# Keys and queries of the split units: each loaded once, to one half of the partitions, two units deep, with the order searched anew

## The chip, the core and the metric

The kernel runs on one core of a Trainium2 chip. The metric is the device time of one execution in microseconds (us), lower is better; the time of a kernel is the median of its runs.

## What is computed

Attention with random features (8 batches, 8 heads, 576 positions, head dimension 64, 128 features), and then a feed-forward layer on its output (4608 tokens, model width 512, inner width 2048, exact GELU), all in fp32. The reference, cut to what matters:

```
q_s, k_s = q * scale, k * scale               # scale = 64 ** -0.25
def phi(x):
    h = einsum('bhsd,md->bhsm', x, omega) - sum(x * x) / 2
    return exp(h - max(h)) / sqrt(m)
q_p, k_p = phi(q_s), phi(k_s)
kv, z = einsum('bhsm,bhsd->bhmd', k_p, v), sum(k_p, axis=2)
x = einsum('bhsm,bhmd->bhsd', q_p, kv) / (einsum('bhsm,bhm->bhs', q_p, z) + 1e-06)
x = x.transpose(0, 2, 1, 3).reshape(4608, 512)
h = x @ w_in
out = (0.5 * h * (1 + erf(h / sqrt(2)))) @ w_out
```

## The kernel before

**Units and blocks.** The attention is cut into 32 units of two heads (four units to a batch), the feed-forward layer into 18 blocks of 256 tokens. Units 0 to 7 are computed in plain fp32 while the weights are loaded. Units 8 to 31, the split units, run beside the feed-forward blocks: TensorE (PE) works through the matmuls of the blocks (`product`, L1201, and `mm2`, L1310 to L1312), and the few matmuls of the units stand between them. Blocks 15 to 17 follow when all units are done.

**A split unit.** `split_pre` loads the transposed keys and queries (64 dimensions by two heads by 576 positions each) into the one tile `xt`. It has 128 partitions, so the 64 dimensions fill a half of them. `load_dup` (L752) loads the keys twice, once to either half, and the queries twice; four DMAs of 288 KB a unit. Then ten tiles of up to 256 positions pass through a ring of three buffers `r`: ScalarE (ACT) rounds all 128 partitions to the high part in fp32r (`x_high`, a CAST, L953), and GpSimd (POOL) puts x minus the high part into the upper half of the buffer (`x_low`, L958). So the lower 64 partitions hold the high part and the upper 64 the low part, and one matmul over 128 partitions (`proj`, L966; `om` holds omega in both halves) adds both. ACT copies a part of the result (`proj_lo`, L970), VectorE (DVE) adds it and takes the maximum (`proj_add`, L975). When the five tiles of the keys or of the queries are through, POOL subtracts the maxima (`shift`, L979), ACT takes the exponential (L787), and the rest of the unit follows: the values in two parts (`v_a` on ACT, `v_b` on DVE, L995), the keys' features in two parts (`k_high` on POOL, L489; `k_low` on DVE, L1003), the products and the division (L1013, L857, L872). There is one buffer for the keys and one for the queries: those of the next unit can be loaded when the last `x_low` of this unit has read them.

**What sets the order.** The program is a list of operations, each with its engine. Every engine issues its operations in the order of a table `RANK`, one number for each operation. SyncE (SP) issues nearly all DMAs in one queue, in that order too: loads of keys, queries and values (`load_vst`, L755; `v_max` on DVE, L1035, reads them first), the transposes of the blocks' input (`block_turn`, L1183) and of the queries' features (`q_turn`, L989), and the stores (L1322). A DMA whose operands aren't ready holds back those behind it. The numbers that stand in the calls of `op` (a cost, and for DMAs `size` and `off`) are the planner's; they choose free buffers for PSUM tiles and add a few filling matmuls at the start, and otherwise cost nothing on the chip.

Of the kernel before, what the change touches and what calls it, by code (L numbers as in the profile page):

```python
# [15 lines left out]
ALU = mybir.AluOpType  # L16
# [19 lines left out]
RANK = (1, 0, 0, 0, 0, 1, 25, 0, 4, 6, 1, 2, 3, 3, 2, 3, 6, 5, 6, 9, 9, 8, 10, 7, 12, 23, 23, 3, 10, 15, 12, 16, 11, 14, 14, 21, 17, 24, 3, 5, 7, 2,  # L36
# [342 lines left out]
def favor_attention_ffn(ctx: ExitStack, tc: tile.TileContext, qT, kT, v, omT, w_in, w_out, out):  # L379
    nc = tc.nc  # L380
    B, H, D, S = qT.shape
    NJ = H // 2
# [366 lines left out]
    def load_dup(u, s):  # L749
        sv = (kT, qT)[s][u.b, 2 * u.j:2 * u.j + 2].rearrange("h d s -> d h s")  # L750
        for r in range(2):
            nc.sync.dma_start(xt[r * D:(r + 1) * D, s], sv)  # L752
# [194 lines left out]
    XG = [(a + g * P, a + min(g + 2, NT) * P) for a in (0, R2) for g in range(0, NT, 2)]  # L947
    NK = len(XG) // 2
    KG = [list(range(g, g + 2)) for a in (0, MID + 1) for g in range(a, a + MID, 2)] + [[MID]]

    def x_high(u, i):
        a, b = XG[i]
        nc.scalar.copy(G['r', u, i][:, 0:b - a], xf[:, a:b])  # L953
# [601 lines left out]
```

## Time and profile before

| | |
|---|---|
| time, median of 3 runs (lowest, highest) | 916.39 us (916.22, 916.94) |
| time of the profiled execution | 916.21 us |
| its span, from the first to the last instruction | 914.4 us |
| busy share: PE, ACT, DVE, POOL | 98%, 81%, 80%, 61% |
| DMA: bytes, share of the 16 engines | 98.95 MB, 47.1% |
| TensorE's granted clock | full speed throughout |

The time of an execution is its span and what lies around it, here 1.8 us. A busy share is the time in which an engine had an instruction under way; matmuls overlap in a pipeline, so PE counts as busy also where its matmuls come a little late. PE does the bulk of the work in nearly all of the span; what the other engines do costs time only where PE waits for it.

### The profile page before, as it was taken

To read this page: it belongs to the slowest core of one execution; us is meant where nothing else is said; L and a number is where in the kernel's file an instruction comes from. 1 tells how busy PE (TensorE), PEld (TensorE's weight loads), DVE (VectorE), ACT (ScalarE), POOL (GpSimd) and SP (SyncE) were. 2 spreads that over 40 slices of the span, in tenths; PEclk is the share of its full clock that TensorE was granted. 3 is DMA by queue.
4 is the path that set the end of the run, shared out by engine and by line. 5 is a ranking of instruction groups with operands and counts; after the bars stand their busy time and mean duration, and the time that the engine had idled before them with its cause. 6 is when DMAs were issued, how large, how long until landed. Compare 5 with 4: busy or idle time off the path is not lost.

```text
span 914.4 us, 26629 instructions
## 1 busy us (share of the span) xinstructions
PE 899.0 (98%) x10037; PEld 699.4 (76%) x10037; DVE 728.3 (80%) x2378; ACT 739.2 (81%) x1590; POOL 556.7 (61%) x809
## 2 busy tenths in 40 slices
PE   8999999999999999999999999999999999999998
PEld 6886777687767777777777777767877877679997
DVE  3877999988988898777767888788879777756665
ACT  6999888999998888987789878989898846555553
POOL 1355568777888566764468636887686416544432
PEclk9999999999999999999999999999999999999999
DMA  9866612649446663484354476384645231121200
GB/s 281 252 211 199 170 43 80 154 93 179 92 102 129 154 123 91 103 184 85 63 140 96 91 148 132 75 173 80 143 101 92 49 74 30 24 54 42 48 25 24
DMA packets 165168, 101.27 MB, mean 111 GB/s; under 512 B 132528, under 2 KB 141104, under 8 KB 165040
## 3 DMA queue, kind: packets, MB, share of 16 engines
q1 hardware_dynamic: 164672, 98.95, 47.1%
q8 instruction: 79, 1.29, 0.6%
q10 hardware_dynamic: 368, 0.62, 0.2%
q14 instruction: 49, 0.40, 0.1%
HBM read 60.36 MB, written 9.44 MB: 76 GB/s over the span
## 4 chain that ended last, share of the span: by engine, by line
PE 89%; ACT 5%; DVE 2%; DMA 2%; issue 1%; POOL 1%; SPq 0%; DVEq 0%; ACTq 0%; POOLq 0%
PE h L1201 33%; PE acc L1310 9%; PE acc L1311 9%; PE acc L1312 9%; PE at L966 5%; PE h L1188 3%; PE acc L1303 3%; PE acc L1265 3%; PE at L857 2%; PE at L1265 2%; PE at L1013 2%; PE at L847 1%; DMA xh<-xc 1%; PE h L794 1%; DMA raw<-in_w_in 1%
## 5 line engine op out<-in xcount | busy, mean ns | idle before, releaser
L958 POOL TENSOR_TENSOR r<-xt,r 64x256 fp32r<-64x256 f32 (+1 forms) x240 | 180.6, 763 | 108.8 <-ACT r L953 81.7
L1201 PE MATMUL h<-xh,w 128*128 128x128 f16 x3264 | 236.2, 219 | 0.0
L1201 PE MATMUL h<-xh,wih 128*128 128x128 f16 x1632 | 197.2, 220 | 1.5 <-DVE h L1218 1.1
L1201 PEld LDWEIGHTS <-w 128*128 128x128 f16 x3264 | 195.6, 98 | 2.8
L1310 PE MATMUL acc<-woh,gh 128*128 128x512 f16 x448 | 170.3, 380 | 0.0
L1311 PE MATMUL acc<-woh,gl 128*128 128x512 f16 x448 | 169.8, 379 | 0.4 <-DVE gl L1300 0.4
L1312 PE MATMUL acc<-wol,gh 128*128 128x512 f16 x448 | 169.8, 379 | 0.0
L1201 PE MATMUL h<-xh,wil 128*128 128x128 f16 x816 | 155.5, 219 | 0.0
L1201 PEld LDWEIGHTS <-wih 128*128 128x128 f16 x1632 | 138.6, 98 | 11.8 <-DVE h L1218 0.9
L1300 DVE SCALAR_TENSOR_TENSOR gl<-h,bs,gh 128x512 f16<-128x512 f32 x116 | 86.3, 746 | 31.8 <-ACT gh L1235 30.6
L966 PE MATMUL at<-om,r 128*128 128x256 f32 x432 | 103.7, 342 | 4.0 <-POOL r L958 2.6
L953 ACT CAST r<-xt 128x256 fp32r<-128x256 f32 (+1 forms) x240 | 90.9, 390 | 13.4 <-PE at L966 9.2
L970 ACT COPY lo<-at 128x256 f32<-128x256 f32 (+1 forms) x240 | 82.3, 354 | 18.0 <-PE at L966 13.6
L1226 ACT ACTIVATE h<-h,bs 128x512 f32<-128x512 f32 x116 | 77.1, 666 | 19.0 <-PE h L1201 15.9
L966 PEld LDWEIGHTS at<-om,r 128*128 128x128 f32 x432 | 70.3, 189 | 23.7 <-POOL r L958 3.7
L1208 ACT COPY g<-h 128x256 f32<-128x256 f32 x136 | 50.6, 373 | 45.8 <-PE h L1201 44.8
L1312 PEld LDWEIGHTS <-gh 128*128 128x128 f16 x464 | 45.4, 98 | 54.5
L1201 PEld LDWEIGHTS <-wil 128*128 128x128 f16 x816 | 80.0, 98 | 7.4 <-issue 1.8
L1235 ACT ACTIVATE gh<-h,bs 128x512 f16<-128x512 f32 x116 | 80.1, 692 | 4.6 <-PE acc L1312 3.4
L1310 PEld LDWEIGHTS <-gh 128*128 128x128 f16 x464 | 45.3, 98 | 35.1 <-issue 0.2
L1213 DVE TENSOR_TENSOR g<-h,g 128x128 f32<-128x128 f32 x136 | 38.8, 285 | 41.3 <-ACT g L1208 40.5
L1311 PEld LDWEIGHTS <-gl 128*128 128x128 f16 x464 | 45.5, 98 | 33.5 <-DVE gl L1300 0.7
(234 smaller groups left out, 2125.0 us busy)
## 6 DMA issues: line engine op xcount, KB each, us to landing
xt<-in_qT SPq DMA_DIRECT2D x56, 288.0 KB, 4.4
xt<-in_kT SPq DMA_DIRECT2D x54, 288.0 KB, 4.3
out_x<-o SPq DMA_DIRECT2D x35, 256.0 KB, 3.1
raw<-in_w_in SPq DMA_DIRECT2D x16, 512.0 KB, 6.2
raw<-in_w_out SPq DMA_DIRECT2D x16, 512.0 KB, 4.4
w<-in_v SPq DMA_DIRECT2D x24, 320.0 KB, 4.2
vt<-in_v SPq DMA_DIRECT2D x8, 320.0 KB, 6.7
qpad<-qc SPq DMA_TRANSPOSE x48, 3.7
```

The lines of the kernel that those rows point to most:

```text
L953: nc.scalar.copy(G['r', u, i][:, 0:b - a], xf[:, a:b])
L958: nc.gpsimd.tensor_tensor(r, xf[D:, a:b], r, op=ALU.subtract)
L966: nc.tensor.matmul(o[:, t], r[:, t * P:(t + 1) * P], om, start=True, stop=True)
L970: nc.scalar.copy(G['lo', u, i][:, 0:n], pp_k(u, i)[:, 0:n, 1])
L1201: nc.tensor.matmul(h, w[p], x[r], start=first and i + m == 0, stop=last and i == 1 and m == 2, skip_group_check=True)
L1208: nc.scalar.copy(G['sa', n, c], G['h', n, c][:, 0:2 * P])
L1226: nc.scalar.activation(h, h, AF.Gelu, scale=G['bs', n][:, 2:3])
L1235: nc.scalar.activation(G['gh', n, c], G['h', n, c], AF.Copy, scale=G['bs', n][:, 3:4])
L1300: nc.vector.scalar_tensor_tensor(G['gl', n, c], G['h', n, c], G['bs', n][:, 3:4], G['gh', n, c], op0=ALU.mult, op1=ALU.subtract)
L1310: nc.tensor.matmul(acc, gh, woh[:, f, c0:c1], start=f == 0, stop=False, skip_group_check=True)
L1311: nc.tensor.matmul(acc, gl, woh[:, f, c0:c1], start=False, stop=False, skip_group_check=True)
L1312: nc.tensor.matmul(acc, gh, wol[:, f, c0:c1], start=False, stop=f == NF - 1, skip_group_check=True)
```

## The change

The keys of a unit are loaded once, to the lower half of the partitions, the queries once, to the upper half (`load_one` in place of `load_dup`): two DMAs of 288 KB a unit instead of four, so 48 DMAs fewer. The space that this leaves holds a second unit: unit k uses the columns `k % 2`, so the loads of one unit wait for the unit before the last. `x_high` now works on 64 partitions, the half in which the data lie, and `x_low` reads that half and writes the low part to the other half of `r`. For the keys the high part is below and the low part above, as before; for the queries it is the other way round. An operation without an engine makes the first split unit's loads wait until all plain units have used `xt`. The planner's numbers for DMAs are changed (larger sizes for transposes, stores and values), and all of `RANK` is new. The instructions of PE are the same in number and shape, those of DVE and POOL too.

```diff
-RANK = (1, 0, 0, 0, 0, 1, 25, 0, 4, 6, 1, 2, 3, 3, 2, 3, 6, 5, 6, 9, 9, 8, 10, 7, 12, 23, 23, 3, 10, 15, 12, 16, 11, 14, 14, 21, 17, 24, 3, 5, 7, 2,
...
-    def load_dup(u, s):
+    def load_one(u, s):
         sv = (kT, qT)[s][u.b, 2 * u.j:2 * u.j + 2].rearrange("h d s -> d h s")
-        for r in range(2):
-            nc.sync.dma_start(xt[r * D:(r + 1) * D, s], sv)
+        nc.sync.dma_start(xt[s * D:(s + 1) * D, u.k % 2], sv)
...
+    def x_cols(u, i):
+        a, b = XG[i]
+        z = i // NK
+        x = xt[z * D:(z + 1) * D, u.k % 2].rearrange("p h s -> p (h s)")[:, a - z * R2:b - z * R2]
+        r = G['r', u, i][:, 0:b - a]
+        return x, r[z * D:(z + 1) * D], r[(1 - z) * D:(2 - z) * D]
+
     def x_high(u, i):
-        a, b = XG[i]
-        nc.scalar.copy(G['r', u, i][:, 0:b - a], xf[:, a:b])
+        x, hi, _ = x_cols(u, i)
+        nc.scalar.copy(hi, x)
 
     def x_low(u, i):
-        a, b = XG[i]
-        r = G['r', u, i][D:, 0:b - a]
-        nc.gpsimd.tensor_tensor(r, xf[D:, a:b], r, op=ALU.subtract)
+        x, hi, lo = x_cols(u, i)
+        nc.gpsimd.tensor_tensor(lo, x, hi, op=ALU.subtract)
...
-            op('SP', 0.5, load_vst, u, r=['vstf'], w=[u.vk], size=340e3, off=2.5)
+            op('SP', 0.5, load_vst, u, r=['vstf'], w=[u.vk], size=400e3, off=2.6)
...
-            op('SP', 1.45, load_dup, u, s, w=[('x', s, a) for a in range(2)], size=720e3, off=3.2)
+            op('SP', 0.75, load_one, u, s, w=[('xp', u.k % 2, s)], size=330e3, off=2.4)
...
-            xr, rk = [('x', i // NK, a) for a in range(2)], ('r', u, i)
+            xr, rk = [('xp', u.k % 2, i // NK)], ('r', u, i)
...
+                if not moved:
+                    op(None, 0, nothing, w=[(x, a, c) for x in ('x', 'xp') for a in range(2) for c in range(2)])
+                    moved = True
```

**The load of the keys of unit 27.** On SP before (the first row is the keys of unit 26, the row `in_kT` in the middle those of unit 27, the last those of unit 28; `w_71<-in_v` is a unit's values):

```order
L752 DMA xt<-in_kT 64x2x576 x2
L989 DMA_TRANSPOSE qpad<-qc 128x9x128
L1322 DMA out_x<-o 128x512 x2
L989 DMA_TRANSPOSE qpad<-qc 128x9x128
L752 DMA xt<-in_qT 64x2x576 x2
L1183 DMA_TRANSPOSE xh<-xc 128x12x128
L752 DMA xt<-in_kT 64x2x576 x2
L755 DMA w_71<-in_v 128x640
L752 DMA xt<-in_qT 64x2x576 x2
L1183 DMA_TRANSPOSE xh<-xc 128x16x128
L989 DMA_TRANSPOSE qpad<-qc 128x9x128 x2
L752 DMA xt<-in_kT 64x2x576 x2
```

The same place now (the first `in_kT` is unit 26, the row `in_kT` with x2 is units 27 and 28):

```order
L751 DMA xt<-in_kT 64x2x576
L994 DMA_TRANSPOSE qpad<-qc 128x9x128 x3
L751 DMA xt<-in_kT 64x2x576 x2
L1327 DMA out_x<-o 128x512
L1188 DMA_TRANSPOSE xh<-xc 128x12x128
L751 DMA xt<-in_qT 64x2x576
L1188 DMA_TRANSPOSE xh<-xc 128x16x128
L994 DMA_TRANSPOSE qpad<-qc 128x9x128 x2
```

The keys of unit 27 stood behind the block's transpose `xh` (128x12x128) and now stand ahead of it, and those of unit 28 moved past both block transposes and two of `qpad`.

**The first tile of unit 27 on ACT.** Before (the first CAST is the last tile of unit 26's queries, the second the first tile of unit 27's keys):

```order
L953 CAST r<-xt 128x128
L1235 ACTIVATE gh<-h,bs 128x512
L1020 COPY kvs<-at 128x128
L1175 ACTIVATE xc<-ts,bs 128x512 x2
L1026 ACTIVATE kvz<-at 128x2
L970 COPY lo<-at 128x256
L1029 ACTIVATE kvh<-kvz 128x130
L953 CAST r<-xt 128x256
L1235 ACTIVATE gh<-h,bs 128x512
```

And now:

```order
L987 ACTIVATE qc<-et 128x1152
L959 CAST r<-xt 64x128
L959 CAST r<-xt 64x256
L975 COPY lo<-at 128x256
L1231 ACTIVATE h<-h,bs 128x512
L975 COPY lo<-at 128x256
L1240 ACTIVATE gh<-h,bs 128x512
L1025 COPY kvs<-at 128x128
L959 CAST r<-xt 64x256
```

Seven instructions stood between the two tiles; now the first tile of unit 27 stands right behind the last of unit 26.

**The values of unit 26.** On SP before (the second `in_v` row here is unit 27, the first unit 26) and on DVE, where `vmax` is the maximum of unit 26's values:

```order
L752 DMA xt<-in_kT 64x2x576 x2
L1183 DMA_TRANSPOSE xh<-xc 128x12x128
L1322 DMA out_x<-o 128x512
L755 DMA w_71<-in_v 128x640
L752 DMA xt<-in_qT 64x2x576 x2
L989 DMA_TRANSPOSE qpad<-qc 128x9x128 x2
L755 DMA w_71<-in_v 128x640
```

```order
L995 SCALAR_TENSOR_TENSOR w_71<-w_71,vsc 128x10x64
L1035 TENSOR_REDUCE vmax<-w_71 128x1
L1300 SCALAR_TENSOR_TENSOR gl<-h,bs,gh 128x512
L1179 SCALAR_TENSOR_TENSOR xc<-ts,bs,xc 128x512
L975 ISA w_71,nm<-at,lo 128x128
```

Now, on SP (the first `in_v` is unit 25, the second unit 26) and on DVE:

```order
L1188 DMA_TRANSPOSE xh<-xc 128x12x128
L751 DMA xt<-in_kT 64x2x576
L754 DMA w_71<-in_v 128x640
L751 DMA xt<-in_qT 64x2x576
L1327 DMA out_x<-o 128x512
L754 DMA w_71<-in_v 128x640
L751 DMA xt<-in_kT 64x2x576
L1188 DMA_TRANSPOSE xh<-xc 128x16x128
```

```order
L1219 TENSOR_TENSOR h<-h,g 128x256
L1028 TENSOR_TENSOR kvz<-at,kvs 128x2x64
L1040 TENSOR_REDUCE vmax<-w_71 128x1
L1223 TENSOR_TENSOR h<-h,g 128x128
L1305 SCALAR_TENSOR_TENSOR gl<-h,bs,gh 128x512
```

The values of unit 26 were loaded behind the keys of unit 24; they now stand ahead of them. On DVE the maximum moved behind the sums `kvz` of a unit.

## Rows read from the trace of the kernel before

**Rows 1.** The page: its span, and each engine's busy time and instructions.

```profile
span 914.4 us, 26629 instructions
...
PE 899.0 (98%) x10037; PEld 699.4 (76%) x10037; DVE 728.3 (80%) x2378; ACT 739.2 (81%) x1590; POOL 556.7 (61%) x809
```

**Rows 2.** Stretches: length, busy PE, PEld, DVE, ACT, POOL, clock, DMA share, GB/s.

```profile
0.00:112.00 112.00, 107.77 (x809) 86.89 (x809) 83.87 (x204) 98.06 (x218) 49.64 (x47) 1.00 0.75 225
112.00:690.00 578.00, 571.41 (x6542) 434.05 (x6539) 487.50 (x1800) 508.97 (x1112) 405.85 (x595) 1.00 0.53 113
...
880.00:914.40 34.40, 30.15 (x380) 28.00 (x377) 20.50 (x46) 15.95 (x33) 10.75 (x18) 0.99 0.09 32
```

**Rows 3.** Waits of PE by what it waited for: total us, times, longest.

```profile
PE at L966 <- POOL r L958: 2.6, 3, 1.5
PE at L966 <- DVE nm L975: 1.4, 1, 1.4
```

**Rows 4.** Timeline, unit 27's first keys: start us, length, engine, instruction [idle before <-releaser].

```profile
597.47 1.29 SPq L752 DMA_DIRECT2D xt<-in_kT  x2
...
602.82 0.41 ACT L953 CAST r<-xt 128x256 fp32r<-128x256 f32 x1 [1.57 <-DMA xt<-in_kT]
...
607.51 3.27 POOL L958 TENSOR_TENSOR r<-xt,r 64x256 fp32r<-64x256 f32 x3
...
608.77 0.38 PE L1311 MATMUL acc<-woh,gl 128*128 128x512 f16 x1
608.98 0.38 PE L1312 MATMUL acc<-wol,gh 128*128 128x512 f16 x1
610.84 0.74 PE L966 MATMUL at<-om,r 128*128 128x256 f32 x4 [1.48 <-POOL r L958]
```

**Rows 5.** Timeline, the values of unit 26 on SP, DVE and PE.

```profile
531.58 0.42 SPq L755 DMA_DIRECT2D w<-in_v  x1
...
536.58 0.82 DVE L1035 TENSOR_REDUCE vmax<-w 128x1 f32<-128x640 f32 x1 [1.68 <-DMA w<-in_v]
...
540.33 0.23 PE L1201 MATMUL h<-xh,wih 128*128 128x128 f16 x1 [0.49 <-DVE h L1218]
...
543.13 0.19 PE L857 MATMUL at<-kvl,qpad 128*128 128x65 f16 x1 [0.31 <-DVE kvl L1032]
...
545.70 0.20 PE L857 MATMUL at<-kvh,qpad 128*128 128x65 f16 x1 [0.22 <-DVE xk L872]
```

**Rows 6.** Timeline, where DVE and POOL overlap, on POOL, DVE and PE.

```profile
549.37 0.88 DVE L995 SCALAR_TENSOR_TENSOR w<-w,vsc 128x640 f16<-128x640 f32 x1
...
556.17 0.22 PE L1201 MATMUL h<-xh,wih 128*128 128x128 f16 x1 [0.64 <-DVE h L1218]
...
683.15 2.11 POOL L979 TENSOR_TENSOR w<-w,nm 128x1152 f32<-128x1152 f32 x1
...
683.30 2.65 DVE L995 SCALAR_TENSOR_TENSOR w<-w,vsc 128x640 f16<-128x640 f32 x1 [0.24 <-ACT w L992]
...
686.71 0.36 PE L966 MATMUL at<-om,r 128*128 128x256 f32 x1 [1.35 <-DVE nm L975]
```

**Rows 7.** Timeline of PE, a wait in the keys of unit 14.

```profile
278.68 0.39 PE L966 MATMUL at<-om,r 128*128 128x256 f32 x1 [0.72 <-POOL r L958]
```

**Rows 8.** DMA: queue's packets, MB, share; issues by tile, KB each, us to landing; landing of L752.

```profile
q1 hardware_dynamic: 164672, 98.95, 47.1%
...
xt<-in_kT SPq DMA_DIRECT2D x54, 288.0 KB, 4.3
...
DMA to landing us min/median/max: 3.5/4.3/6.9
```

**Rows 9.** Groups by shape on POOL and timeline of ACT: work on fewer and more partitions.

```profile
L958 POOL TENSOR_TENSOR r<-xt,r 64x256 fp32r<-64x256 f32 x192 | 153.7, 807 | 81.2 <-ACT r L953 60.8 <-issue 7.9 <-POOL w L489 2.2
...
L1152 POOL TENSOR_TENSOR ts<-xk 128x256 f32<-128x256 f32 x34 | 27.5, 814 | 3.9 <-DVE w L617 1.7 <-DVE xc L1179 1.2
...
269.00 0.20 ACT L499 COPY bs<-bs 32x5 f32<-32x5 f32 x1
269.23 0.19 ACT L500 COPY bs<-bs 64x5 f32<-64x5 f32 x1
```

More of the change, by code (lines that the diff above doesn't have):

```diff
@@ L31 @@
 X = dict(pm=0.15, tsw=1.28, psw=0.057, pst=0.3, plain=8, tiles=6, fill=0.6, kvp=8, eb0=8, amax=0, ahead=4.5)
-RANK = (1, 0, 0, 0, 0, 1, 25, 0, 4, 6, 1, 2, 3, 3, 2, 3, 6, 5, 6, 9, 9, 8, 10, 7, 12, 23, 23, 3, 10, 15, 12, 16, 11, 14, 14, 21, 17, 24, 3, 5, 7, 2,
[173 rows of a table removed]
+RANK = (1, 0, 0, 0, 0, 1, 41, 0, 4, 6, 1, 2, 2, 3, 3, 3, 6, 6, 4, 9, 8, 8, 7, 7, 14, 17, 21, 3, 9, 16, 12, 19, 10, 15, 17, 24, 18, 26, 3, 5, 10, 2, 7,
[173 rows of a table added]
 PO = {}
@@ L1121, in split_post @@
         for a in range(2):
-            op('SP', 1.35, q_turn, u, a, r=[qc] + [qc + (1,)] * a, new=[(('qf', 'ql')[a], (('qf', 'ql')[a], u))], size=600e3, off=1.7)
+            op('SP', 1.35, q_turn, u, a, r=[qc] + [qc + (1,)] * a, new=[(('qf', 'ql')[a], (('qf', 'ql')[a], u))], size=740e3, off=1.7)
         out_ops(u)
@@ L1353, in block_prep @@
                 op('SP', 1.55, block_turn, n, k, r=[xc] + [xc + (q, l) for q in (p - 1, p) for l in range(2)] + [('xh', n)] * k, w=[('xh', n, k)],
-                   new=[] if k else [('xh', ('xh', n))], size=(800e3, 1060e3)[k], off=1.7)
+                   new=[] if k else [('xh', ('xh', n))], size=(950e3, 1250e3)[k], off=1.7)
     def ffn_first(n, c):
@@ L1416, in ffn_second @@
                             op('DVE', 0.12 + (min(c1, end) - c0) / 960, o_last, n, i, c0, min(c1, end), r=[('acc', n, 2 + i, 0)], w=[('o', n, i, c0)] + [('o', n, i)] * (n < NBLK - 1))
-                        op('SP', 0.45, store_dma, n, i, c0, c1, r=[('o', n, i), ('o', n, i, c0)], size=270e3 * (c1 - c0) / DM)
+                        op('SP', 0.45, store_dma, n, i, c0, c1, r=[('o', n, i), ('o', n, i, c0)], size=300e3 * (c1 - c0) / DM)
             return
@@ L1429, in ffn_second @@
                        new=[] if c0 else [('o', ('o', n, i))], due=(1, n + 1, (lag + i * .6) / nc_, 0.0), kind='F' if n >= N32 else 'F0')
-                    op('SP', 0.45, store_dma, n, i, c0, c1, r=[('o', n, i)], size=270e3 * (c1 - c0) / DM, due=(1, n + 1, (lag + 1) / nc_, 0.0))
+                    op('SP', 0.45, store_dma, n, i, c0, c1, r=[('o', n, i)], size=300e3 * (c1 - c0) / DM, due=(1, n + 1, (lag + 1) / nc_, 0.0))
     def p2():
@@ L1484, in favor_attention_ffn @@
     op('DVE', 0.2, vb_ones, w=['vb'])
-    done_u = NJ
+    done_u, moved = NJ, False
     for n in range(1, NBLK):
@@ L1501, in favor_attention_ffn @@
         if n == min(SB):
-            op(None, 0, nothing, w=[('et', e, t) for e in range(2) for t in range(2 * NT)] + [('x', a, c) for a in range(2) for c in range(2)]
+            op(None, 0, nothing, w=[('et', e, t) for e in range(2) for t in range(2 * NT)] + [('xp', a, c) for a in range(2) for c in range(2)]
                + [('vst', i) for i in range(NVS)] + ['kk', 'vb', 'tgf'] + [('kk', g) for g in range(len(KG))])
```

346 rows, old and new, of the table RANK are left out of this document.

## The prediction

> **What bounds the kernel now.** I read the page first, then PE busy time by stretches, then PE's waits, then the timeline ahead of each wait, back to what was late first. The page says that PE is busy for 899.0 us of a span of 914.4 us [rows 1]. The other engines are at 61% to 81%, so their work costs time only where PE stands still for it. The change leaves PE's instructions as they are in number and shape; all that it can win or lose is in the 15.4 us in which PE isn't busy, and in how late matmuls come inside the busy time.
>
> By stretches [rows 2]: in the first 112 us (plain units, weights) PE lacks 112.00 - 107.77 = 4.23 us, most of it at the very start. From 112 to 690 us, where the split units run beside the blocks, it lacks 578.00 - 571.41 = 6.59 us. From 880 us it lacks 34.40 - 30.15 = 4.25 us, the last store's way out. The change works in the middle stretch, so 6.59 us is what it can win there as idle time. An idle stretch costs a little more than it is long: ahead of the wait at 610.84 us PE's matmuls start 0.21 us apart (608.77, 608.98), and the next one starts 1.86 us later [rows 4]. That is 1.65 us lost for 1.48 us shown; I add 0.16 us to each wait. Some 14 waits make the most that the middle can give 6.59 + 14 x 0.16 = 8.8 us (an estimate; the count is mine from the timeline).
>
> Who is waited for: `proj` for the subtraction on POOL, 2.6 us in three waits, and for DVE's maxima, 1.4 us in one [rows 3]. Both are ends of chains, so I went back in time from the largest.
>
> Chain 1, 1.48 us at 610.84 us [rows 4]. The keys of unit 27 are issued at 597.47 us. ACT reaches their first tile and stands 1.57 us until 602.82 us for the DMA. POOL's subtractions for the following tiles end at 607.51 + 3.27 = 610.78 us, and PE goes on 0.06 us later. A DMA was late by about as much as PE then waited.
>
> Chain 2, 0.49 + 0.31 + 0.22 us from 540.33 us [rows 5]. The values of unit 26 are issued at 531.58 us; DVE stands 1.68 us for them until 536.58 us, and what is queued behind (the sums `h` that PE needs, then `kvl`, then the division) is late three times.
>
> Two others have nothing to do with loads [rows 6]. At 683.15 us POOL begins a `shift` of 2.11 us, and DVE's `v_b`, which takes 0.88 us at 549.37 us, takes 2.65 us from 683.30 us. PE then waits 1.35 us at 686.71 us. The 0.64 us at 556.17 us stands likewise behind a DVE instruction beside a `shift`. The 0.72 us at 278.68 us [rows 7] I couldn't trace to one cause.
>
> **The change part by part.**
>
> Removed: 48 of the 96 loads of 288 KB, 48 x 0.295 = 14.2 MB of the 98.95 MB on the queue, one seventh; the DMA engines are busy 47.1% [rows 8]. By itself that is worth nothing, since no load is on PE's path but through the two chains. For those it matters: loads land 3.5 to 6.9 us after issue, 4.3 in the median [rows 8], and the pair of 597.47 us took over 5 us.
>
> Moved, on SP and ACT: the order shows the keys of unit 27 ahead of the block's transpose that they stood behind; with a second buffer nothing forbids that. SP then goes past no new wait for a buffer, since the unit before the last has been read long ago. The keys of chain 1 were 1.57 us late. Now they are one load instead of a pair, whose issue alone holds SP for 1.29 us [rows 4], and the transpose that held them back stands behind them; I judge that to be more than 1.57 us, and take chain 1 away whole: 1.48 + 0.16 = 1.64 us. The same on ACT: the first tile of unit 27 now comes right behind the last of unit 26, seven instructions earlier, so that a late load there would again hold up ACT; it would have to be late by those seven too.
>
> The values of unit 26 stand ahead of the keys of unit 24 now, and DVE takes their maximum after more work. I take chain 2 away whole: 0.49 + 0.31 + 0.22 + 3 x 0.16 = 1.50 us. What is late next in either place is the ordinary mix, which I leave as it is.
>
> Changed in kind: 240 CASTs on ACT cover 64 partitions instead of 128, and 240 subtractions on POOL write to the other half. Length goes by the columns, not the partitions: POOL's tensor_tensor over 256 columns takes 807 ns on 64 partitions and 814 ns on 128, ACT's copy of 5 columns 0.20 us on 32 and 0.19 us on 64 [rows 9]. So nothing for ACT; a gain is excluded by that row. For POOL no row shows a write to other partitions than those read. I take nothing, since it is the same operation over the same columns; the bounds are nothing and twice the 807 ns (below). What covers it: POOL is busy 405.85 of 578 us [rows 2].
>
> The wait before the first split unit: its loads now wait for all plain units' queries too. It lies ahead of 112 us, where PE has the plain feed-forward block to do, and PE shows no wait for those loads; nothing, or the few tenths of a small wait.
>
> Everything else is the new order: who stands beside whom in 112 to 690 us is drawn again. The waits that aren't from loads, 6.59 - 1.48 - 1.02 = 4.09 us, may shrink or grow; I take them as equal, as I do the start's 4.23 us and the end. The largest is of a kind the order still holds: a `v_b` somewhere beside a `shift`.
>
> Sum: 916.21 us (this execution) - 1.64 - 1.50 = 913.07 us. It lies 0.18 us below the median of the runs, which gives **913.2 us**. I call under 0.2% (1.8 us) no change, about what a measurement of this kernel can tell.
>
> **The rivals.**
>
> *The loads are gone but other waits take their place: about 915.8 us.* Four waits of chain 2's sort, 0.5 us each with its 0.16, give back 4 x 0.66 = 2.6 us. For it: 4 us of the middle's idle time has no load in it, and PE at 99% is waiting for whoever is last. Against it: the two largest load waits are named and both have a place in the order that moved.
>
> *DVE behind `shift`: slower.* POOL runs 48 shifts of 2.1 us; two of them now end in a wait of PE, 1.35 and 0.64 us, mean 1.0 and 1.15 us with its start-up. The Trainium skill (SBUF — State Buffer, "Who interferes with whom") says that a VectorE instruction with two SBUF inputs and a GpSimd instruction that reads SBUF exclude each other for the whole instruction, whoever came first; this trace agrees, with 2.65 us in place of 0.88. Where the new order leaves n shifts with PE's next operand behind them, the time is 913.2 + (n - 2) x 1.15. It comes out above 918.2 us, slower by over 0.2%, from n = 7; at n = 8 it is 920.1 us. For it: the same pair, `v_b` and `shift`, stands in every unit. Against it: only two of 48 cost PE anything.
>
> *The subtraction across halves is slow.* If a write to the other half took twice 807 ns, POOL would have 240 x 0.8 = 194 us more; 405.85 + 194 = 600 us doesn't fit in the 578 us of the middle. POOL would be the bound there, and 22 us plus the waits of a full engine would be added: some 945 us. The Trainium skill (GPSIMD Engine Reference, "Extended-addressing connectivity") speaks for it: in a tensor_tensor each core works on its own 16 partitions. No run here shows such a write.
>
> *More than the loads' waits goes.* If an order with later loads no more in its way also halves the other 4.09 us: 913.2 - 2.0 - 0.16 x 4 = 910.5 us; with all gone, 908 us.
>
> **How the numbers follow.** Load waits gone, the rest as before, 912 to 914.5: 0.38. More gone, 908 to 912: 0.20. Given back, 914.6 to 918.2: 0.24. Shifts, 918.2 to 921: 0.14. POOL slow: 0.04. So faster by over 0.2% is 0.38 + 0.20 = 0.58, within 0.2% is 0.24, slower 0.18. The likeliest alone is 912 to 914.5 us. The range runs from 908.5, near the most that the middle can give (916.4 - 8.8 = 907.6), to 919.0: it leaves out the slow POOL, most of the shifts' case, and a few in a hundred below.
>
> **What would show it.** Right: ACT no longer waits for `xt` from 112 to 690 us; DVE's wait for values is gone; PE's idle time in the middle stretch falls from 6.6 to about 4 us; POOL's subtraction of 256 columns stays near 807 ns. Wrong: PE's waits behind DVE (`nm`, `h`, `gl`) grow beside a `shift`; POOL's subtraction is longer; ACT waits for `xt` at tiles that were moved forward; or the start loses more than 4.2 us, since pieces of the weights and values there are in another order too.

## The result, and the profile after

The changed kernel takes 923.17 us (median of 4 runs, 922.41 to 924.62) against 916.31 us for the kernel before in the same comparison: a ratio of 1.0076, 95% interval 1.0058 to 1.0093. It is slower by 6.9 us where 913.2 us was predicted, and lies outside the range. The profiled execution took 922.41 us.

The head of the page of the changed kernel, which answers to [rows 1]:

```profile
span 920.6 us, 26586 instructions
...
PE 903.4 (98%) x10037; PEld 703.2 (76%) x10037; DVE 732.6 (80%) x2378; ACT 756.0 (82%) x1590; POOL 557.9 (61%) x809
```

The counts of PE, ACT, DVE and POOL are those of before, and one figure stands out: ACT is busy for 756.0 us, 16.8 us more than the 739.2 us of [rows 1], with the same 1590 instructions. DVE and PE gained about 4 us each, POOL 1. I had costed the change at nothing for ACT.

The stretches of [rows 2] after (us, busy us of each engine with its instructions, granted clock, DMA share, GB/s):

```profile
0.00:112.00 112.00, 108.15 (x787) 87.46 (x788) 78.84 (x201) 95.61 (x213) 48.84 (x48) 0.97 0.77 225
112.00:690.00 578.00, 569.10 (x6478) 431.99 (x6477) 489.92 (x1778) 520.47 (x1100) 401.76 (x588) 1.00 0.41 90
```

Two things: in the first 112 us the granted clock is 0.97 where it was full before, and in the middle PE lacks 578.00 - 569.10 = 8.90 us where it lacked 6.59 us, instead of the 4 us that I expected. To place the loss I set the k-th matmul of each kind in the one trace against the k-th of the same kind in the other. The first matmul of the plain feed-forward block starts 2.95 us later (57.6 us in before), the matmul that started at 159.6 us still 2.96 us later, the last one 6.23 us later. So about 3.0 us are lost in the first 58 us, nothing from there to 159.6 us, and 3.3 us behind that. The 3.0 us are not idle time: in the first 112 us PE lacks 112.00 - 108.15 = 3.85 us, less than the 4.23 us of before.

The start, by single microseconds (us, PE busy us with its matmuls, granted clock, DMA share, GB/s):

```profile
14.00:15.00 1.00, 0.11 (x2) 1.00 1.10 375
15.00:16.00 1.00, 1.00 (x9) 0.85 1.13 294
16.00:17.00 1.00, 1.00 (x6) 0.50 1.07 270
...
21.00:22.00 1.00, 1.00 (x8) 0.50 0.14 51
22.00:23.00 1.00, 1.00 (x8) 0.74 0.00 0
23.00:24.00 1.00, 1.00 (x11) 1.00 0.00 0
```

From 15.7 to 22.5 us TensorE runs at 0.50, the lower of its two levels (1.2 GHz), and gets 6 to 8 matmuls done in a microsecond. Before, the same microseconds, behind a wait as long (0.91 us, to 0.89 us after), are at 1.00, with 11 matmuls:

```profile
14.00:15.00 1.00, 0.10 (x1) 1.00 1.12 383
15.00:16.00 1.00, 0.99 (x9) 1.00 1.06 344
16.00:17.00 1.00, 1.00 (x11) 1.00 1.08 389
```

PE's waits in the middle (us in total, times, longest), which answer to [rows 3]:

```profile
PE h L1206 <- DVE h L1223: 3.0, 3, 1.4
PE acc L1316 <- DVE gl L1305: 1.2, 1, 1.2
PE at L971 <- POOL r L963: 1.1, 2, 0.9
PE at L1018 <- DVE nm L980: 0.8, 1, 0.8
PE h L1206 <- DVE gl L1305: 0.8, 2, 0.5
```

The waits for POOL's subtraction have gone down from 2.6 to 1.1 us, and DVE no longer waits for values; the load chains of the prediction are gone. ACT still waits for keys once, 2.2 us at the first split unit (until 121.73 us), and PE has no wait behind it. Waits for DVE have taken their place. The largest, 1.24 us at 581.89 us and 1.42 us at 605.54 us, look like the rival "DVE behind `shift`". DVE at the first of them:

```profile
578.95 0.43 DVE L1219 TENSOR_TENSOR h<-h,g 128x256 f32<-128x256 f32 x1
579.29 2.34 DVE L1008 SCALAR_TENSOR_TENSOR w<-w 128x256 f16<-128x256 f32 x1
581.55 0.28 DVE L1223 TENSOR_TENSOR h<-h,g 128x128 f32<-128x128 f32 x1
```

and POOL beside it:

```profile
579.24 2.11 POOL L984 TENSOR_TENSOR et<-et,nm 128x1152 f32<-128x1152 f32 x1
```

The split of the keys' features (`k_low`, L1008), 0.42 us in the median of its kind, takes 2.34 us, and the addition that PE needs stands behind it. So my first theory, **O**, was that the new order costs the time, at the start by the clock and in the middle by DVE beside POOL. Its rival, **L**, was that the loads, or the write to the other half, cost it.

### The profile page after: what moved, and what is told of

It is laid out like the page before. It is cut to its first block, busy times and chain, and to the rows that moved or that the text cites. A ratio compares the mean times of both kernels' runs of the same rounds, so it can differ in the third digit from the quotient of the medians.

```text
span 920.6 us, 26586 instructions
## 1 busy us (share of the span) xinstructions
PE 903.4 (98%) x10037; PEld 703.2 (76%) x10037; DVE 732.6 (80%) x2378; ACT 756.0 (82%) x1590; POOL 557.9 (61%) x809
## 4 chain that ended last, share of the span: by engine, by line
PE 83%; ACT 8%; DVE 4%; issue 2%; DMA 2%; POOL 1%; SPq 0%; DVEq 0%; ACTq 0%; POOLq 0%
PE h L1206 30%; PE acc L1315 8%; PE acc L1316 8%; PE acc L1317 8%; PE at L971 5%; PE h L1193 3%; PE acc L1308 3%; PE acc L1270 3%; PE at L1270 2%; PE at L1018 2%; PE at L856 2%; PE at L846 1%; PE h L793 1%; ACT r L959 1%; ACT lo L975 1%
## 5 line engine op out<-in xcount | busy, mean ns | idle before, releaser
L963 POOL TENSOR_TENSOR r<-xt,r 64x256 fp32r<-64x256 f32 (+1 forms) x240 | 176.3, 743 | 103.3 <-ACT r L959 65.4
L971 PE MATMUL at<-om,r 128*128 128x256 f32 x432 | 106.1, 346 | 2.0 <-POOL r L963 1.1
L959 ACT CAST r<-xt 64x256 fp32r<-64x256 f32 (+1 forms) x240 | 89.5, 381 | 17.7 <-PE at L971 8.8
L975 ACT COPY lo<-at 128x256 f32<-128x256 f32 (+1 forms) x240 | 80.4, 350 | 8.7 <-PE at L971 3.1
L980 DVE CUSTOM_DVE_ANT_0 w<-at,lo 128x128 f32<-128x128 f32 x198 | 48.8, 285 | 20.4 <-ACT lo L975 19.0
```

Source lines behind the costliest of these rows:

```text
L959: nc.scalar.copy(hi, x)
L963: nc.gpsimd.tensor_tensor(lo, x, hi, op=ALU.subtract)
L971: nc.tensor.matmul(o[:, t], r[:, t * P:(t + 1) * P], om, start=True, stop=True)
L975: nc.scalar.copy(G['lo', u, i][:, 0:n], pp_k(u, i)[:, 0:n, 1])
```

## The experiments

The runs were made in four groups: e1 to e5, e6 to e9, e10 to e13, e14 to e16. Each group has runs of the kernel before, with medians of 916.1 to 917.1 us; the ratios and their 95% intervals are to those. Differences between my kernels are those of their medians, so across groups a difference below 1 us isn't certain.

**e1_loads_only**: the new loads, and every engine in the order of before.

```diff
-RANK = (1, 0, 0, 0, 0, 1, 41, 0, 4, 6, 1, 2, 2, 3, 3, 3,
+RANK = (1, 0, 0, 0, 0, 1, 25, 0, 4, 6, 1, 2, 3, 3, 2, 3,
...
```

> The new loads with the order of before: every engine issues its work in the order of the kernel before, and only what the loads and the split write is new. Theory O (the new order costs the time, the loads do not): the load waits of before (1.48 us at 610.84, 1.02 us between 540 and 546) go at least in part, the clock stays at 1.00 throughout, 913.5 to 916.5 us. Theory L (the loads or the write to the other half cost it): 920 to 923 us.

Measured: 924.45 us (923.47 to 925.35), 1.0079 times before, 1.0064 to 1.0094. Theory O falls: with the order of before the kernel is as slow as the changed one. Two of the five runs have a mean clock of 0.995 (925.3 us), three 0.999 (923.5 to 924.5 us); the clock is the smaller part here. Since the order is the same, every instruction has its counterpart in before, and the lateness could be followed along ACT. It grows by some 0.12 us at a time, mostly at a query's CAST and at the instruction right behind it (185 of the 243 steps above 0.08 us). These are the rows of ACT in the changed kernel where that shows, a cast of a key piece first (lower half), then one of a query piece (upper half):

```profile
594.61 0.28 ACT L959 CAST r<-xt 64x128 fp32r<-64x128 f32 x1
594.80 0.36 ACT L1213 COPY g<-h 128x256 f32<-128x256 f32 x1
595.06 0.36 ACT L975 COPY lo<-at 128x256 f32<-128x256 f32 x1
595.45 0.40 ACT L959 CAST r<-xt 64x256 fp32r<-64x256 f32 x1
595.88 0.37 ACT L975 COPY lo<-at 128x256 f32<-128x256 f32 x1
```

The first number is the start, the second the length. Behind the key cast the next instruction starts at 594.80 us, 0.09 us before the cast's end at 594.89 us. The query cast waits for the end of the COPY ahead of it (595.06 + 0.36 = 595.42, then 0.03 us), and the COPY behind it waits for the cast's end (595.85, then 0.03 us). In before, with casts over 128 partitions:

```profile
217.99 0.39 ACT L953 CAST r<-xt 128x256 fp32r<-128x256 f32 x1
218.28 0.36 ACT L970 COPY lo<-at 128x256 f32<-128x256 f32 x1
218.55 0.40 ACT L953 CAST r<-xt 128x256 fp32r<-128x256 f32 x1
```

That is a CAST every 0.56 us with a COPY between. I then took all pairs of the changed kernel in which ACT did not have to wait (at most 40 ns idle). A cast on the lower half starts 104 ns before the end of a neighbour on all partitions (median; 84 of 89 overlap), and the neighbour behind it 97 ns before the cast's end (82 of 83). For casts on the upper half both are 24 ns behind the end (none of 94 and none of 89 overlap). Two casts on the upper half in a row overlap again (9 of 9, by 93 ns). So the length of an instruction is what I said, 0.40 us in either kernel; its price is not: 104 + 24 + 97 + 24 = 249 ns more for each of the 120 query casts, at most 30 us of ACT's time. This is theory **S**. Its rival **W** is that POOL and DVE waiting for each other cost the time whatever ACT does.

**e8_upper_cast** and **e9_lower_cast** test that in the kernel before, with its loads and its order, where both halves of `xt` hold the same data. The diff is that of e8; e9 has `:D` and `D:` exchanged in the new lines.

```diff
     def x_high(u, i):
         a, b = XG[i]
-        nc.scalar.copy(G['r', u, i][:, 0:b - a], xf[:, a:b])
+        nc.scalar.copy(G['r', u, i][D:, 0:b - a], xf[D:, a:b])

     def x_low(u, i):
         a, b = XG[i]
-        r = G['r', u, i][D:, 0:b - a]
-        nc.gpsimd.tensor_tensor(r, xf[D:, a:b], r, op=ALU.subtract)
+        r = G['r', u, i][:, 0:b - a]
+        nc.gpsimd.tensor_tensor(r[:D], xf[D:, a:b], r[D:], op=ALU.subtract)
```

> The kernel before (its loads, its order), but every one of its 240 casts runs on partitions 64 to 127 alone, and POOL writes the low part to partitions 0 to 63. Theory S: twice as many such casts as in e1_loads_only, so about twice its 7.2 us: 926 to 933 us. If a half cast costs ACT nothing: 916 to 917.5 us.

> The kernel before, but every one of its 240 casts runs on partitions 0 to 63 alone, and POOL reads there and writes the low part to partitions 64 to 127. Theory S: casts that begin at partition 0 overlap as before, and POOL's write to the other half costs nothing: 916 to 917.5 us. If any half cast, or POOL's write to the other half, costs: as e8_upper_cast.

Measured: e8 934.65 us (1.0194, 1.0179 to 1.0209), e9 915.81 us (0.9992, 0.9983 to 1.0001). The two differ in nothing but the half, by 18.8 us for 240 casts. ACT in e8:

```profile
221.32 0.40 ACT L953 CAST r<-xt 64x256 fp32r<-64x256 f32 x1
221.74 0.37 ACT L970 COPY lo<-at 128x256 f32<-128x256 f32 x1
222.14 0.40 ACT L953 CAST r<-xt 64x256 fp32r<-64x256 f32 x1
```

and in e9, at the same place of the program:

```profile
217.79 0.39 ACT L953 CAST r<-xt 64x256 fp32r<-64x256 f32 x1
218.08 0.36 ACT L970 COPY lo<-at 128x256 f32<-128x256 f32 x1
218.35 0.40 ACT L953 CAST r<-xt 64x256 fp32r<-64x256 f32 x1
```

A cast and a copy take 0.82 us in e8 and 0.56 us in e9. Theory S is shown, and POOL's write to the other half, which both have, costs nothing: e9 is no slower than before. That POOL writes up in the one and down in the other makes no difference either: a subtraction takes 747 ns in e8 and 756 ns in e9.

**e7_old_order_full_cast** takes the price out of e1_loads_only: the query cast covers all 128 partitions (the lower half of what it writes is overwritten by POOL's low part), and six matmuls keep the clock up (e4_fill_wait, below).

```diff
     def x_high(u, i):
         x, hi, _ = x_cols(u, i)
+        if i >= NK:
+            a, b = XG[i]
+            x, hi = xt[:, u.k % 2].rearrange("p h s -> p (h s)")[:, a - R2:b - R2], G['r', u, i][:, 0:b - a]
         nc.scalar.copy(hi, x)
```

> The new loads with the order of before, as e1_loads_only, with the cast of the queries over 128 partitions and the six matmuls at 14 us. Theory S: of the 7.2 us that e1_loads_only lost behind 160 us nearly all comes back, and the loads give at most the 1.6 + 1.0 us of the waits that they end: 914 to 917 us. Rival W, or loads that cost by themselves: 921 to 924 us.

Measured: 915.51 us (0.9991, 0.9982 to 1.0000), 8.9 us below e1_loads_only, or 8.1 us by the two ratios. The new loads by themselves are worth 0.6 us, and the interval reaches from nothing to 1.6 us. ACT's wait of 1.57 us at the head of chain 1 is gone, but PE's wait there is still 0.78 us long after 1.48 us: 3 us later ACT waits 1.20 us for DVE's `dn` (the denominators of the division).

**e3_old_start** and **e4_fill_wait** are about the start. e3 issues what the changed kernel planned for its first 58 us in the order of before, the rest in the new one; here the first rows of SP that this moves:

```diff
 L743 DMA vt_74<-in_v 128x10x64
-L559 DMA raw<-in_w_in 128x4x256 x2
-L747 DMA xt<-in_kT 128x576 x2
 L743 DMA vt_75<-in_v 128x10x64
 L559 DMA raw<-in_w_in 128x4x256 x2
-L747 DMA xt<-in_qT 128x576
 L747 DMA xt<-in_kT 128x576
+L747 DMA xt<-in_qT 128x576 x2
+L747 DMA xt<-in_kT 128x576
+L559 DMA raw<-in_w_in 128x4x256 x2
...
```

e4 keeps the new order and adds six matmuls ahead of the first `kv`, whose results are overwritten:

```diff
-        if X['fill'] and o.idle > 0.9 and o.t > 5.0:
+        if X['fill'] and (o.idle > 0.9 and o.t > 5.0 or o.id == 23):
...
-            for _ in range(int((o.idle - 0.3) * X['fill'] / 0.11) if t else 0):
+            for _ in range(6 if o.id == 23 else int((o.idle - 0.3) * X['fill'] / 0.11) if t else 0):
```

> The changed kernel, but what it did in its first 58 us is issued in the order of before; the rest keeps the new order. If the new order of the start is what let the clock fall: granted clock 1.00 from 16 to 22 us and 923.2 - 3.0 = 920.2 us. If the fall has nothing to do with the order there: clock 0.50 again and 923 us.

> The changed kernel with six matmuls more (128x256 bf16, results overwritten, about 0.13 us each) in front of the first L793, in the wait of 0.89 us at 14.0. If that wait is what lets the clock fall at 15.85 us: clock 1.00 there and 920.2 us. If what TensorE did earlier decides it: clock 0.50 again, 923 us.

Measured: e3 919.23 us (1.0023, 1.0013 to 1.0032), e4 920.23 us (1.0034, 1.0021 to 1.0047), both with a mean clock of 0.999 to 1.000 in every run. So the fall of the clock goes with what TensorE does in the wait of 0.89 us at 14.0 us. It is not certain in that order: e5_comb_first has the same start, and two of its six runs show 0.993 and 0.994 (924.7 us), four 0.998 to 1.000 (919.8 to 921.3 us). Nor is the order of before free of it: the profile of e1_loads_only shows 0.50 for 6.8 us from 17.2 us, and six of the 62 runs of the kernel before in the four groups have a mean clock of 0.995 or 0.996 (918.2 to 919.3 us). In e4, at full clock, the matmul that started at 57.6 us still comes 1.5 us late, in e3 0.3 us early: half of the start's 3.0 us is the clock, half the order.

**e5_comb_first**: at the two places beside a shift the addition that PE waits for goes ahead of the DVE instruction that the shift holds up, `k_low` at the first, as in the diff, and `block_low`, the low part of a block's input, at the second (2.47 us at 602.81 us).

```diff
 L1219 TENSOR_TENSOR h<-h,g 128x256
-L1008 SCALAR_TENSOR_TENSOR w_71<-w_71 128x256
-L1223 TENSOR_TENSOR h<-h,g 128x128
+L1223 TENSOR_TENSOR h<-h,g 128x128
+L1008 SCALAR_TENSOR_TENSOR w_71<-w_71 128x256
```

> The changed kernel with two DVE instructions of one kind moved: at 579 and at 602 us the last addition on h (L1223) stands ahead of the DVE split that ran beside a shift of POOL (2.34 us at 579.29, 2.47 us at 602.81). If the DVE instruction held beside the shift is what TensorE waits for: the waits of 1.24 and 1.42 us go and the time is 923.2 - 2.7 = 920.5 us. If another wait takes their place: 922 to 923.5 us.

Measured: 921.11 us (919.82 to 924.83), with the clock's two kinds of runs mixed. In the profiled run both waits are gone, but 0.68 us for `gl` and 0.80 us for the values' split `v_b` stand right behind them: `k_low` still takes 2.00 us beside the shift, and what is queued behind it is next. From the matmul of 569.5 us in before to that of 631.9 us the kernel gains 0.20 us on before, where the changed kernel lost 0.52 us: 0.7 us of the 2.7 us expected. The time shows no gain: the four runs near full clock lie about e4's 920.2 us.

**Theory S in the new order.** Three attempts to take the price out there failed to tell. **e6_full_cast** is e4 with e7's cast; in **e10_full_cast_other_slot** the queries lie in the columns `(u.k + 1) % 2`, beside the next unit's keys; **e11_full_cast_comb_first** is e10 with e5's two moves. The line that e10 changes beside e7's:

```diff
-        nc.sync.dma_start(xt[s * D:(s + 1) * D, u.k % 2], sv)
+        nc.sync.dma_start(xt[s * D:(s + 1) * D, (u.k + s) % 2], sv)
```

> The kernel of e4_fill_wait (changed kernel, clock kept at 1.00 by six matmuls), and ACT's cast of a query piece runs over all 128 partitions again (the lower half of the result is overwritten by POOL's low part) where the change casts partitions 64 to 127 alone. Theory S (an ACT instruction on the upper half does not overlap with its neighbours on all partitions: 24 ns behind their end where the others start about 100 ns ahead of it, so about 0.25 us for each of 120 casts, some 30 us of ACT): casts overlap again, and 913 to 917 us, against 920.2 us. Rival W (what is lost is lost to POOL and DVE waiting for each other, whatever ACT does): 919.5 to 921 us.

> The kernel of e4_fill_wait (new loads, new order, clock kept at 1.00), the cast of the queries over all 128 partitions as in e6_full_cast, but the queries of a unit lie beside the keys of the next unit, so that the cast doesn't wait for keys that take the place of its own unit's. If e6_full_cast lost its time to ACT waiting for keys (13.0 us in three waits), and theory S holds in the new order too: those waits are gone, casts overlap, 913 to 917 us. If the new order itself costs what was lost: 919 to 921 us.

> e10_full_cast_other_slot with the two DVE instructions of e5_comb_first moved ahead of the splits that stood beside a shift: where those two waits of 1.2 and 1.4 us are still there, 2.6 us below e10_full_cast_other_slot; where ACT's earlier casts have moved the shifts away, no difference.

Measured: 933.94, 932.65 and 932.28 us. A cast over 128 partitions also reads the keys that lie below the queries, and in the new order, where a unit is loaded up to two units ahead, those are just being loaded. ACT's waits for keys in e6 and in e10, 112 to 690 us, where the changed kernel has 2.2 us in one:

```profile
ACT r L962 <- DMA xt<-in_kT: 13.0, 3, 5.5
```

```profile
ACT r L962 <- DMA xt<-in_kT: 20.1, 7, 4.5
```

In all three the clock fell too, in spite of the six matmuls: in the profiles once, at 612 us, in e6, three times in e10 (20.5 us at 0.50 in all) and four times in e11, there already at 11.0 us. So these runs measure new waits and a lower clock, and say nothing for or against S; e11 can't be told from e10. Keys and queries of two units on the lower half, which would be the clean remedy, would double the 9.2 KB of a partition that `xt` takes, and weren't tried.

**e14_new_order_lower** and **e15_new_order_upper** avoid the wait: the queries' casts and subtractions read data that are never loaded again, in e14 on the lower half, as in the diff, in e15 on the upper (`:D` and `D:` exchanged). Both leave the queries out of the result: their loads stay, but nothing waits for them. Both have the six matmuls of e4.

```diff
+    def y_cols(u, i):
+        n = XG[i][1] - XG[i][0]
+        r = G['r', u, i][:, 0:n]
+        return vt[0].rearrange("p n d -> p (n d)")[:D, 0:n], r[:D], r[D:]
...
+        if i >= NK:
+            x, hi, _ = y_cols(u, i)
```

> The kernel of e4_fill_wait (new loads, new order). The 120 casts of query pieces, and the subtractions behind them, read the values of the first unit (which stay where they are) on partitions 0 to 63 in place of the queries on 64 to 127, and write cast and low part to the halves that the keys use: the queries are left out of the result, their loads stay but nothing waits for them. Theory S in the new order: without the casts on the upper half some of the 3.7 us by which e4_fill_wait lies above the kernel before go, and the gain of the loads shows: 913 to 917 us, and at least 3 us below e15_new_order_upper. If the order costs it: as e15_new_order_upper, 919 to 921 us.

> The same as e14_new_order_lower in all but the half: the casts read the values of the first unit on partitions 64 to 127, as the queries lay (the queries are left out here too). What e14_new_order_lower and this one share, loads that nothing waits for, is thus taken out of their difference. By both theories near e4_fill_wait: 919 to 921 us.

Measured: e14 913.83 us (0.9964, 0.9952 to 0.9975), e15 921.03 us (1.0045, 1.0032 to 1.0057). The half alone makes 7.2 us (a subtraction on POOL takes 741 and 742 ns); on the whole page ACT is busy for 736.5 us in e14 and 756.2 us in e15. e15 stands near e4 (1.0034). The middle stretch of e14:

```profile
112.00:690.00 578.00, 573.85 (x6566) 436.13 (x6565) 490.40 (x1801) 508.32 (x1117) 407.56 (x600) 1.00 0.42 90
```

and of e15:

```profile
112.00:690.00 578.00, 568.84 (x6473) 431.13 (x6472) 488.63 (x1776) 520.52 (x1100) 401.52 (x588) 1.00 0.41 90
```

PE lacks 4.15 us in e14 and 9.16 us in e15, for 12 us of ACT's busy time. PE's waits in e14:

```profile
PE h L1215 <- DVE h L1232: 1.6, 2, 1.2
PE acc L1325 <- DVE gl L1314: 1.2, 1, 1.2
PE at L980 <- POOL r L972: 0.5, 1, 0.5
```

The wait behind the shift at 581.89 us is still there (1.19 us), the one at 605.54 us is not: one of the two was DVE beside a shift, the other, though beside a shift as well, came only with ACT's lateness.

**e12_values_earlier, e13_split_after_shift, e16_before_two_moves** test the prediction's own terms in the order of before. e12 is e7 with the values of unit 26 moved ahead on SP; e13 is e12 with the split of the values of unit 28 moved behind the next maxima on DVE; e16 is the kernel before with these two moves alone.

```diff
 L751 DMA xt<-in_kT 64x2x576
+L754 DMA w_71<-in_v 128x640
 L1191 DMA_TRANSPOSE xh<-xc 128x12x128
 L1330 DMA out_x<-o 128x512
-L754 DMA w_71<-in_v 128x640
...
 L1222 TENSOR_TENSOR h<-h,g 128x256
+L1226 TENSOR_TENSOR h<-h,g 128x128
+L983 ISA w_71,nm<-at,lo 128x128
...
 L1003 SCALAR_TENSOR_TENSOR w_71<-w_71,vsc 128x10x64
-L1226 TENSOR_TENSOR h<-h,g 128x128
-L983 ISA w_71,nm<-at,lo 128x128
...
```

> The kernel of e7_old_order_full_cast (915.5 us) with one load moved: the values of unit 26 stand ahead of the block's transpose and a store on SP. By the prediction's chain 2: DVE's wait of 1.82 us at 536 us is gone, and PE's waits of 0.50, 0.31 and 0.21 us behind it, 1.0 to 1.5 us: 914.0 to 914.5 us. If PE's three waits have another cause: 915.5 us.

> e12_values_earlier with one DVE instruction moved: the split of the values (2.64 us at 682.67, beside a shift of POOL from 682.52) stands behind the next maxima. If being held beside the shift is the price: PE's wait of 1.35 us at 686 us is gone, 1.35 to 1.5 us below e12_values_earlier, 912.5 to 913.2 us. If not: the time of e12_values_earlier.

> The kernel before with only the two moves of e12_values_earlier and e13_split_after_shift, and its own loads. If those two moves make nearly all of e13_split_after_shift's gain: 916.4 - 1.0 - 1.4 = 914.0 us, and the new loads are worth the 0.7 us at 610 us that is left to 913.1 us. If the moves need the new loads: 915 to 916.5 us.

Measured: e12 914.50 us (0.9978, 0.9968 to 0.9987), e13 913.12 us (0.9963, 0.9951 to 0.9975), e16 914.16 us (0.9969, 0.9957 to 0.9981). DVE reads the values of unit 26 without a wait, where it stood 1.68 us before [rows 5], and the split off the shift is 0.88 us long again, where it took 2.65 us [rows 6]. From e12:

```profile
534.13 0.88 DVE L1003 SCALAR_TENSOR_TENSOR w<-w,vsc 128x640 f16<-128x640 f32 x1
534.93 0.81 DVE L1043 TENSOR_REDUCE vmax<-w 128x1 f32<-128x640 f32 x1
```

and from e13:

```profile
684.58 0.88 DVE L1003 SCALAR_TENSOR_TENSOR w<-w,vsc 128x640 f16<-128x640 f32 x1
```

e13 beats both kernels, by 3.4 us and 10 us; e16 shows that most of that needs none of the new loads: e13, which has them, lies 1.0 us below it, or 0.5 us by the two ratios, and the two intervals overlap.

## Why the prediction was wrong

**The step that failed** is "Changed in kind": "Length goes by the columns, not the partitions ... So nothing for ACT". The length was right (403 ns for 256 columns in the changed kernel, 411 ns before). What ACT pays for an instruction is when the next one may start, and that row can't show it. I compared the lengths of two copies [rows 9] and not their starts with the ends of their neighbours. A CAST and a COPY of before start 0.29 us apart at a length of 0.39 us, and I didn't ask what that overlap hangs on. The two copies had the answer beside them. They are those of `spread`, which write partitions 32 to 63 and 64 to 127, and these are their neighbours on all partitions in before:

```profile
266.85 2.13 ACT L787 ACTIVATE et<-et 128x2304 f32<-128x2304 f32 x1
...
269.45 1.12 ACT L1175 ACTIVATE xc<-xk,bs 128x256 f16<-128x256 f32 x2
```

The first copy starts at 269.00 us, 0.02 us behind the end at 268.98 us; the second ends at 269.42 us, 0.03 us ahead of the next start (which reads what it wrote, so the first is the cleaner case). In the whole trace of before none of 22 such starts and one of 20 such ends overlaps (at most 40 ns idle, as above), while a copy of two columns on all partitions (L1026) starts ahead of its neighbour's end in 18 of 19 cases. So the price could have been asked for before the change was run. The cost is 7.2 us in the new order (e15 against e14), 8.9 us in that of before (e1 against e7, 0.6 us of it the clock, by e1's three runs with a mean clock of 0.999, 923.8 us in the median).

The Trainium skill (Perfetto Trace Analysis, "Optimizing Scalar/DVE Operations") says that the fixed overhead of such an instruction appears in its profiled latency at about twice what it costs the engine, since the half of it that waits for the write's acknowledgement overlaps with the next instruction. This trace agrees for neighbours on all partitions and on the lower half (97 to 104 ns of overlap) and not where one of two neighbours covers the upper half alone (24 ns behind the end).

**The second miss** is the start's 4.23 us, which the prediction took "as equal". It cost 3.0 us in the profiled run, half by the order of its first 58 us, half by the clock. The prediction named it among what would make it wrong, and gave it no price; and the sign that it named, more than 4.2 us lost there, would not have shown it, since PE's idle time there fell to 3.85 us. The Trainium skill (TensorE: Matmul & The Clock Gate, "Part 1: The HAM clock gate") says that the clock follows what TensorE did before. The runs here agree: of the new order's start without the six matmuls, six runs of ten have a mean clock of 0.993 to 0.997 (all four of the changed kernel, two of e5's six), with them none of 16 (0.999 to 1.000 in e4, e14 and e15).

**What was right.** Without the upper casts the amount in the middle is as predicted: PE's idle time there is 4.15 us (about 4 expected), and from 159.6 us to the end e14 gains 1.25 + 2.26 = 3.5 us on before, where the sum said 3.14. That the two agree so closely is in part luck. The waits that the prediction kept are not the ones that are left: the 1.35 us for `nm` at 686.71 us is gone, and 1.2 us for `gl` and 1.2 us beside a shift have come. And e14 waits for no queries, so its gain is not that of the loads and the order alone. POOL's write to the other half is free: 743 ns a subtraction (763 before). The sum with the two misses: 916.2 + 3.0 - 3.5 + 7.2 = 922.9 us, for 923.2 measured. The low end of the range rested on 14 waits in the middle; the trace of before has 10 above 0.15 us, which would make 8.2 us of the 8.8, and nothing came near it.

**Right in mechanism, off in size:** chain 1, 1.64 us, gave 0.6 to 0.7 us, since DVE's `dn` was late right behind the load; chain 2, 1.50 us, gave 1.0 us (e12 against e7). And neither is the worth of the load's new form: the loads alone gave 0.6 us, and chain 2 goes with one DMA moved in the old kernel. **The rival DVE behind `shift`** forecast a slower kernel, as measured, but with the wrong cause. Its price holds (1.4 us for one instruction moved off a shift, e13 against e12; 1.15 was said), but of PE's waits in the changed kernel only the two shown above are of that kind, and one of them went with ACT's lateness; seven were needed.

Left open: how the 3.5 us of e14 divide between the loads, the order and queries that nothing waits for, since the old loads were not run in the new order; and which property of the upper half stops the overlap. It isn't the upper half as such, for the copies that write partitions 32 to 63 lose the overlap too. A start away from partition 0 would fit all these rows, but that is a guess: only the two halves were compared by runs.

## What to carry to other kernels

Cost an instruction by the distance from its start to that of the next one on its engine, not by its length, and read that distance for the very neighbours it will have: a change of partitions alone can end an overlap of 0.1 us on either side. On an engine busy for 80% of the time, 20 us of such losses (756.2 against 736.5 us busy) cost the kernel 7 us. Where two engines are drawn into a new order, price the start too: a wait there that TensorE survived at full clock may not be survived the next time. Six matmuls in it kept the clock in 16 runs of 16 of e4, e14 and e15; they are no cover against a fall elsewhere, as e6, e10 and e11 show.

## What was not expected of the hardware

An ACT instruction on partitions 64 to 127 and a neighbour on all 128 do not overlap (0 of 183 pairs, 24 ns behind the end), one on partitions 0 to 63 and such a neighbour do (166 of 172 pairs, by about 100 ns), and two on the upper half do (9 of 9); all these are casts of the changed kernel. A subtraction on POOL that reads one half and writes the other is as fast as one that stays in its half, 743 and 763 ns. TensorE's clock fell to 0.50 for 6.8 us behind a wait of 0.89 us, in some runs of a kernel and not in others: six of ten runs with the new order's start have a mean clock of 0.997 or less, and six of 62 runs of the kernel before one of 0.996 or less, though its waits in the first 15 us are nearly the same.
